# Last expert by streamed weights, two narrower expert passes, and one product of the last stage moved ahead of four transpositions

## The chip, the core and the metric

The kernel runs on one core of one Trainium2 chip, as one program that is launched once. The metric is device time in microseconds from the start of an execution to its end: 778.91 us is the median of three runs before the change (778.0 to 779.42). The engines meant below are PE (TensorE; PEld is its weight load, which overlaps its matmuls), DVE (VectorE), ACT (ScalarE), POOL (GpSimd) and SP (SyncE, which here issues most transfers). Each engine works through its own instructions in the order in which the program lists them.

## The reference

Three stages follow each other: attention, a mixture of eight experts of which each token takes one, and a dense layer with a rational function in the middle.

```python
e_idx = np.argmax(x @ w_gate, axis=1)          # x: 2304 tokens x 512, from the attention
for e in range(8):
    mask = e_idx == e
    h = np.maximum(x[mask] @ w1[e], 0.0)       # 512 -> 1024
    ye = h @ w2[e]                             # 1024 -> 512
    out[mask] = gate_w[mask, None] * eom[mask, e, None] * ye
...
h = x @ w_in                                   # 512 -> 2048
g = (a0 + a1*h + a2*h*h + a3*h**3) / (1 + |b0|*|h| + |b1|*h*h + 1e-6)
return g @ w_out                               # 2048 -> 512
```

How many tokens an expert gets follows from the inputs. With the reference's own inputs (seed 0) the eight counts are 422, 331, 253, 249, 220, 149, 434 and 118.

## The kernel before

**Precision.** Every float32 operand of a product is split in two parts, `hi` (a cast) and `lo` (the rest), and a product is made of three matmuls, hi·hi, hi·lo and lo·hi. So weights and tokens both pass an ACT cast and a subtraction on DVE or POOL before PE reads them.

**An expert pass, `wide(e, n, x, bg)`.** The tokens of expert e lie transposed in `x` (512 features by n tokens). The weights are the stationary operand, 128 columns at a time, and the n tokens are the moving one: 8 groups of 12 matmuls into `ph` (first layer) and 8 groups of 12 into four accumulators `acc` (second layer), 192 pairs of a weight load and a matmul in all, whatever n is. ACT makes the rectified `hT` of each `ph`, DVE its lo part. The width n is `WIDE.get(e, BASE)`: 296, 332, 256, 256, 256, 256, 308, 256 for the experts 0 to 7. Tokens beyond n are handled by `beyond(e)`, which stands behind a branch on the count; for the experts 0 and 6, whose tokens beyond the width are prepared in advance, it runs `single`.

**`single(e, to, x, at)`** does 128 tokens the other way round: the tokens are stationary and the weights stream past as the moving operand, 512 columns at a time (or 2 x 256 in its second half with `parts=2`): 24 matmuls for the first layer, 24 (or 48) for the second, three sets of four transpositions, and ACT and DVE work between them. Nothing is woven into it.

**What is woven into a pass.** While pass e runs, `todo` issues step by step (the table `PLANW`, 32 steps): the split of the next expert's 16 weight pieces (`s`; one ACT cast and one subtraction on DVE or POOL, alternating), the gather, scaling and transposition of the next tokens (`g`, `x`, `p`), and `c`, the conversion of 18 pieces of the last stage's weights (three DVE operations and two or three transfers each; `NCONV = 9` operations, three pieces, in each of the passes 1 to 6). Raw weights arrive in a ring of four buffers, `raw`; a buffer's next load is issued by SP once both halves in it are split.

**The last pass.** Pass 7 splits the 16 pieces of `w_in` into slot 0. `first_steps` is woven in too: it splits the first 512 tokens of the last stage (`x2_prep`, four of them, on ACT and DVE), makes the products 0 and 1 of the last stage (24 matmuls, 512 wide, into two `pt` banks) and their rational function (`first_elem`: five ACT, one POOL and five DVE operations each, then a cast and a subtraction). After the pass come `first_product(0)` (the last stage's product 2), the split of the first two pieces of `w_out` (`first_w`), a branch, and `first_product(1)`.

**The last stage** (`moe2`) has 80 steps s. PE alternates between `gemm1(s+2)`, 12 matmuls into one of two `ph` banks in the first 16 steps, and `gemm2`, which needs the finished function values. `elem(s)` is the chain on ACT, POOL and DVE between the two. A `ph` bank is free for the next product when DVE has done its second operation on it.

The functions that the change touches, as profiled:

Of the kernel before, what the change touches and what calls it, by code (L numbers as in the profile page):

```python
# [42 lines left out]
READY, WIDE = (6,), {0: 296, 1: 332, 6: 308}  # L43
# [13 lines left out]
NPRE, NCONV = 2, 9  # L57
# [3 lines left out]
PLANW = plan(32, s=range(0, 31, 2), c=(2, 3, 4, 12, 13, 14, 22, 23, 24), g=(1, 3, 18, 24), x=(1, 2, 14, 16), p=(5, 8, 19, 22))  # L61
PLANW7 = plan(30, s=(0, 5, 6, 8, 9, 11, 12, 14, 15, 17, 18, 20, 21, 23, 24, 25))
# [38 lines left out]
MODE7 = ("act",) + ("act_pool",) * 15  # L101


class Build:
# [731 lines left out]
    def experts(self, st, first, gate):  # L836
# [38 lines left out]
        def single(e, to, x, at=0, put=None, parts=2):  # L875
# [86 lines left out]
        def todo(e, plan, half=None, blocks=(), gathers=(), mode=SPLIT_MODE):  # L962
# [3 lines left out]
            k = NCONV * (e - 1)  # L966
# [26 lines left out]
        blocks = lambda e, bs=range(4): [(e, b, b) for b in bs if e < E]  # L993

# [29 lines left out]
        def expert(e, early=lambda: ()):  # L1024

            plan = PLANW if e < E - 1 else PLANW7
            more_ = blocks(e + 1, (2, 3)) if e + 1 in READY else [None] * 2
            wide(e, wd(e), X(e), weave(todo(e, plan, None, blocks(e + 1, (0, 1)) + more_, more_ + blocks(e + 2, (0, 1))),
# [65 lines left out]
        def first_steps(at=None):  # L1094

            def tick(n):
                while at and at[0] < n:
                    at[0] += 1
                    yield
            for n in range(CH[0]):  # L1100
                yield from tick(1 + n)
                self.x2_prep(n, self.x2c, n)
            h = [ps_t().tile([128, 4, 128], F32, tag="pt", name="pt").rearrange("p c t -> p (c t)") for _ in range(2)]
            gens = [self.first_elem(k, h[k], hr[k]) for k in range(2)]
            order = [("m", 0), ("m", 0), ("e", 0), ("m", 1), ("m", 1), ("e", 0), ("e", 1), ("e", 0), ("e", 1), ("e", 1)]
            parts = [self.product_parts(h[k], self.x2c, k, 512) for k in range(2)]
            for i, (c, k) in enumerate(order):
                yield from tick(8 + i + i // 2)
                next(parts[k] if c == "m" else gens[k], None)
            for k, t in enumerate(GT + (30, 30)):  # L1110
                yield from tick(t)
                next(gens[k % 2], None)
# [357 lines left out]
```

## Time and profile before

| what | value |
|---|---|
| median of the runs shown | 778.91 us |
| the profiled execution, its own time | 779.69 us |
| its span, first to last instruction | 778.0 us |
| PE busy in the span | 757.1 us (97%) |
| granted TensorE clock, mean of the span | 0.993 |
| passes 4 and 5 (experts 4 and 5), from PE's first matmul to the next pass's | 23.70 and 25.10 us |
| from pass 7's first matmul, with the block of expert 6 in it, to the last stage's first `gemm2` | 49.72 us |

The span is what the trace shows. The execution's own time is 1.7 us longer, and the median of the runs lies 0.8 us below that, so a change of the span is carried over to the median as a difference. Idle time of an engine counts only where another one waits for it; PE is the one that is nearly always busy, but what holds it back differs from stage to stage.

### The profile page before, as it was taken

The numbers are of one execution on the slowest core, as the hardware profiler recorded it, in microseconds if no ns is written. First come the engines' busy times: TensorE is split into PE (matmuls) and PEld (weight loads), VectorE is DVE, ScalarE is ACT, GpSimd is POOL, SyncE is SP. The second block draws the span as 40 slices with busy tenths as digits, with TensorE's granted clock in tenths as the row PEclk, the third lists the DMA queues.
The fourth block names the chain that finished last, engine by engine and source line by source line (L and its number), as shares of the span: only waits on it lengthen the run. The fifth ranks groups of instructions, "written<-read, shape, count | busy, mean of one in ns | idle before, by whom it ended". The sixth has DMA issues, their size and how long they took to land. (4 is left out here: it accounts for less than half of the span.)

```text
span 778.0 us, 16683 instructions
## 1 busy us (share of the span) xinstructions
PE 757.1 (97%) x5976; PEld 652.5 (84%) x5976; DVE 584.4 (75%) x1419; ACT 527.3 (68%) x1181; POOL 352.7 (45%) x439
## 2 busy tenths in 40 slices
PE   8998999899999999999999999999999999999996
PEld 5776776698999999998978888898888898989984
DVE  5777788683568877772389998888888768997983
ACT  4666775555455656643778887778777767887872
POOL 4445664523255556541756866532342214322422
PEclk9999999999999999999999999999999999999998
DMA  8998885555588999893463340110010000000101
GB/s 290 323 312 273 291 269 144 144 168 184 191 279 285 316 304 334 287 306 114 127 195 109 109 108 1 51 45 14 1 54 14 1 1 27 28 1 1 40 1 40
DMA packets 51978, 112.55 MB, mean 145 GB/s; under 512 B 10194, under 2 KB 24274, under 8 KB 49832
## 3 DMA queue, kind: packets, MB, share of 16 engines
q1 hardware_dynamic: 42232, 96.39, 39.1%
q0 software_dynamic: 3168, 9.27, 3.4%
q10 hardware_dynamic: 6480, 5.65, 2.3%
q8 instruction: 52, 0.85, 0.5%
q14 instruction: 46, 0.38, 0.2%
HBM read 93.58 MB, written 18.77 MB: 144 GB/s over the span
## 5 line engine op out<-in xcount | busy, mean ns | idle before, releaser
L1256 POOL TENSOR_TENSOR q<-q,ab 128x384 f32<-128x384 f32 (+1 forms) x78 | 93.9, 1204 | 212.1 <-ACT q L1255 205.1
L1295 PE MATMUL acc<-slot,gh 128*128 128x512 f32 x528 | 165.7, 394 | 0.0
L699 POOL TENSOR_TENSOR slot<-raw,slot 128x512 fp32r<-128x512 f32 x66 | 90.3, 1377 | 89.0 <-ACT slot L695 86.9
L1150 PE MATMUL ph<-x2c,slot 128*128 128x512 f32 (+1 forms) x552 | 125.1, 374 | 0.9 <-DVEq L1126 0.6
L1150 PEld LDWEIGHTS ph<-x2c,slot 128*128 128x128 f32 x552 | 101.1, 187 | 19.6 <-DVEq L1126 0.9
L1295 PEld LDWEIGHTS acc<-slot,gh 128*128 128x128 f32 x528 | 98.3, 187 | 20.1 <-ACT gh L1267 0.2
L944 PE MATMUL acc<-hT,slot 128*128 128x256 f32 (+3 forms) x768 | 109.2, 292 | 0.0
L1295 PE MATMUL acc<-slot,gl 128*128 128x512 f32 x264 | 104.4, 395 | 0.0
L944 PEld LDWEIGHTS acc<-hT,slot 128*128 128x128 f32 x768 | 101.9, 189 | 0.2
L695 ACT CAST slot<-raw 128x512 fp32r<-128x512 f32 x128 | 75.0, 618 | 7.6 <-DVE yt L950 4.0
L316 POOL TENSOR_SCALAR pr<-ex,r 128x128 f32<-128x128 f32 x128 | 47.0, 379 | 60.8 <-PE sc L263 21.0
L1150 PE MATMUL ph<-xa,slot 128*128 128x384 f32 x384 | 71.8, 336 | 0.0
L1150 PEld LDWEIGHTS ph<-xa,slot 128*128 128x128 f32 x384 | 67.9, 188 | 2.7
L1267 ACT CAST gh<-u 128x384 fp32r<-128x384 f32 (+1 forms) x78 | 43.3, 555 | 39.0 <-PE acc L1295 20.8
L699 DVE TENSOR_TENSOR slot<-raw,slot 128x512 fp32r<-128x512 f32 x62 | 55.0, 890 | 14.9 <-ACT slot L695 14.4
L1270 ACT ACTIVATE r<-q,cab 128x384 f32<-128x384 f32 (+1 forms) x78 | 51.3, 657 | 19.3 <-POOL q L1256 18.7
L937 ACT ACTIVATE hT<-ph 128x256 fp32r<-128x256 f32 (+3 forms) x64 | 25.7, 401 | 50.8 <-PE ph L932 40.1
L1295 PEld LDWEIGHTS acc<-slot,gl 128*128 128x128 f32 x264 | 49.4, 187 | 12.3 <-DVE gl L1268 0.3
L298 ACT ACTIVATE ex<-sm,mx 128x128 f32<-128x128 f32 x128 | 50.3, 395 | 13.9 <-POOL pr L316 7.0
L1255 ACT ACTIVATE q<-ab,cab 128x384 f32<-128x384 f32 (+1 forms) x78 | 58.3, 747 | 0.9
L1255 ACT ACTIVATE u<-ph,cab 128x384 f32<-128x384 f32 (+1 forms) x78 | 55.0, 705 | 4.0 <-POOL gl L1268 2.8
L932 PE MATMUL ph<-xa,slot 128*128 128x256 f32 (+1 forms) x384 | 54.6, 292 | 1.2 <-PEq L1040 0.4
(235 smaller groups left out, 1471.0 us busy)
## 6 DMA issues: line engine op xcount, KB each, us to landing
raw<-in_w_dram SPq DMA_DIRECT2D x78, 512.0 KB
vw<-in_vw_dram SPq DMA_DIRECT2D x16, 1024.0 KB
r<-in_w_dram SPq DMA_DIRECT2D x18, 512.0 KB
kw<-in_kw_dram SPq DMA_DIRECT2D x16, 384.0 KB
raw<-wf SPq DMA_DIRECT2D x9, 512.0 KB
qt<-in_qT_dram SPq DMA_DIRECT2D x32, 128.0 KB
xbuf<-xrow SPq DMA_DIRECT2D x8, 512.0 KB
xg<-ybuf SPq DMA_DIRECT2D x13, 256.0 KB
```

What stands on the lines that cost most here:

```text
L298: nc.scalar.activation(ex[:, h], src[:, h], AF.Exp, bias=mx[:, h:h + 1], scale=-1.0, accum_out=ssum[:, h:h + 1])
L316: nc.gpsimd.tensor_scalar(out=pr[:, h], in0=ex[:, h], scalar1=r[:, h:h + 1], scalar2=1.0, op0=ALU.mult, op1=ALU.mult)
L695: nc.scalar.copy(hi, r)
L699: eng.tensor_tensor(out=lo[:, c], in0=r[:, c], in1=hi[:, c].bitcast(F32), op=ALU.subtract)
L932: nc.tensor.matmul(ph, lhsT=W[:, b, 2 * k + s // 4, c:c + 128], rhs=x[:, a, k, :n], start=(i == 0), stop=(i == 11))
L944: nc.tensor.matmul(acc[m][:, :n], lhsT=W[:, b, 8 + f, 128 * m:128 * m + 128], rhs=hT(f % nh, n)[:, a], start=(f == 0 and i == 0), stop=(f ...
L1150: self.nc.tensor.matmul(ph[:, :w], lhsT=l[a], rhs=r[b], start=(k == 0 and i == 0), stop=(k == 3 and i == 2))
L1255: nc.scalar.activation(o_, x_, AF.Identity, scale=k1, bias=k0)
L1256: nc.gpsimd.tensor_tensor(out=q, in0=q, in1=ab, op=ALU.mult)
L1267: nc.scalar.copy(g[0], up)
L1270: nc.scalar.activation(r0, q, AF.Ln, bias=eps1)
L1295: nc.tensor.matmul(accs[i], lhsT=l[a], rhs=Wo[:, b, f, :], start=(f == 0 and j == 0), stop=(f == 15 and j == 2))
```

## The change

1. **Widths.** The passes 4 and 5 become 224 and 160 wide instead of 256. Expert 7 is prepared for 128 tokens: `pair(7)` names one block instead of two, so one gather, one scaling and one set of four transpositions with its split go from the passes 5 and 6.
2. **Conversions.** The 18 pieces are spread 4, 3, 3, 2, 2, 4 over the passes 1 to 6 instead of 3 each.
3. **Expert 7.** Its wide pass goes. After pass 6, `beyond(6)` runs at once (before, it ran after the first 12 matmuls of pass 7), and then `single(7)` with `parts=1`, into which `todo` and `first_steps` are woven by a new argument `bg`. The products 0 and 1 go into `acc3` and `acc1`, and `first_elem` keeps |h| in `yt`.
4. **Product 2** (`first_product(0)`) is issued in `single(7)` by `between`, after the second layer and ahead of the last four transpositions.
5. **Split of `w_in`**: `MODE7` gives 6 of the 16 subtractions to DVE and 10 to POOL (before: 1 and 15).

```diff
-READY, WIDE = (6,), {0: 296, 1: 332, 6: 308}
+READY, WIDE = (6,), {0: 296, 1: 332, 4: 224, 5: 160, 6: 308, 7: 128}
...
-NPRE, NCONV = 2, 9
+NPRE = 2
+PIECES = 0, 4, 3, 3, 2, 2, 4, 0
...
-PLANW7 = plan(30, s=(0, 5, 6, 8, 9, 11, 12, 14, 15, 17, 18, 20, 21, 23, 24, 25))
+PLANW7 = plan(20, s=(0, 0, 3, 3, 4, 5, 8, 9, 14, 15, 16, 16, 17, 17, 18, 18))
+ORDER1 = ((4, "m", 0), (5, "m", 0), (7, "e", 0), (8, "m", 1), (10, "e", 0), (11, "m", 1), (11, "e", 0), (12, "e", 1),
+          (13, "e", 0), (14, "e", 0), (14, "e", 1), (15, "e", 1))
...
-        def single(e, to, x, at=0, put=None, parts=2):
+        def single(e, to, x, at=0, put=None, parts=2, bg=iter(()), between=lambda: None):
...
                     if i % 3 == 2:
                         hook(n, i // 3)
+                        if i < 11:
+                            next(bg, None)
                 nc.scalar.activation(hr[n], ph, AF.Relu)
+                next(bg, None)
...
                 for k in ks:
                     hook(2, k)
+                    next(bg, None)
...
             nc.vector.tensor_copy(y[:, 256:], py[-1][:, w - 256:w])
+            between()
             pt = ps_t().tile([128, 4, 128], F32, tag="pt", name="pt")
...
+        def product_0():
+            self.bank = [ps_h.tile([128, 512], F32, tag="ph", name="ph") for _ in range(PRE)]
+            self.first_product(0)
...
         expert(E - 2, early)
-        expert(E - 1, lambda: first_steps([0]))
+        beyond(E - 2)
+        side = weave(todo(E - 1, PLANW7), first_steps([0]))
+        single(E - 1, 0, X(E - 1), parts=1, bg=side, put=put_last, between=product_0)
+        for _ in side:
+            pass
         beyond(E - 1)
-        self.bank = [ps_h.tile([128, 512], F32, tag="ph", name="ph") for _ in range(PRE)]
         first_w()
-        self.first_product(0)
```

PE, in the middle of pass 7 before: the rows L932 and L944 are the pass's own first and second layer, 256 wide, and L1150 is half of product 0 or 1.

```order
L932 MATMUL ph<-xa,slot_3377 128x256 x12
L944 MATMUL acc_6760<-hT_3406,slot_3377 128x256 x3
L944 MATMUL acc_6761<-hT_3406,slot_3377 128x256 x3
L1150 MATMUL pt<-x2c,slot_81 128x512 x6
L944 MATMUL acc_6762<-hT_3406,slot_3377 128x256 x3
L944 MATMUL acc_6763<-hT_3406,slot_3377 128x256 x3
L1150 MATMUL pt<-x2c,slot_81 128x512 x6
```

PE after the change, from behind the block of expert 6 to the end of `single(7)`: L901 is the first layer, L914 the second, L889 and L925 transpositions, L1182 the products 0 (acc_7024), 1 (acc_7071) and 2 (`ph`).

```order
L901 MATMUL acc_6986<-slot_3377,xa 128x512 x12
L901 MATMUL acc_7018<-slot_3377,xa 128x512 x3
L1182 MATMUL acc_7024<-x2c,slot_81 128x512 x6
L901 MATMUL acc_7018<-slot_3377,xa 128x512 x3
L889 MATMUL pt<-ident,hr_3407 128x128 x4
L1182 MATMUL acc_7024<-x2c,slot_81 128x512 x6
...
L1182 MATMUL acc_7071<-x2c,slot_81 128x512 x6
L914 MATMUL acc_7065<-slot_3377,hT_3406 128x512 x12
L1182 MATMUL ph<-x2c,slot_81 128x512 x12
L925 MATMUL pt<-ident,hr_3407 128x128 x4
```

The 192 matmuls of pass 7 are replaced by 48 wider ones, and the first half of product 0 now stands behind 15 matmuls instead of some 90.

ACT after the change, the first rows at the same place: L701 casts pieces of `w_in`, L1221 casts of the last stage's tokens, L906 the rectified first layer, L815 the casts of its transposed form, L1198 the first operation of product 0's function.

```order
L701 CAST slot_81<-raw_74 128x512 x2
L1221 CAST x2c<-xg_90 128x4x128
L1221 CAST x2c<-xg_91 128x4x128
L1221 CAST x2c<-xg_3385 128x4x128
L906 ACTIVATE hr_3407<-acc_6986 128x512
L701 CAST slot_81<-raw_75 128x512 x2
L1221 CAST x2c<-xg_3386 128x4x128
L701 CAST slot_81<-raw_76 128x512
L815 CAST hT_3406<-pt 128x256 x2
L701 CAST slot_81<-raw_76 128x512
L906 ACTIVATE hr_3408<-acc_7018 128x512
L1198 ACTIVATE yt<-acc_7024 128x512
```

Six pieces, four casts of tokens and four operations of expert 7 itself stand ahead of the first operation of product 0's function, and each of expert 7's waits for PE.

ACT before the change, its last rows before the last stage: L695 casts pieces of `w_in`, L1182 casts the two functions, L950 copies the pass's result, L952 and L869 are its transfers, L1117 splits `w_out`.

```order
L695 CAST slot_81<-raw_77 128x512 x2
L1182 CAST xa<-xg_91 128x2x256
L1182 CAST xa<-xg_3386 128x2x256
L950 COPY yt<-acc_6760 128x256
L950 COPY yt<-acc_6762 128x256
...
L952 DMA toks<-idxT 9x128
...
L869 DMA ybuf<-yt 128x4x256
...
L1117 CAST slot_3377<-raw_74 128x512 x2
```

The same place after the change: L920 and L926 copy the expert's result, L1146 and L875 are its transfers, L1214 is the cast of product 1's function, L1137 the split of `w_out`, L1285 the first operation of `elem(2)`.

```order
L920 COPY hr_3407<-acc_7065 128x256
L926 COPY hr_3408<-pt 128x512
...
L1146 DMA toks<-idxT 9x128
...
L875 DMA ybuf<-hr_3408 128x4x128
L701 CAST slot_81<-raw_75 128x512 x2
L1214 CAST xa<-xg_3386 128x2x256
L701 CAST slot_81<-raw_76 128x512 x2
L701 CAST slot_81<-raw_77 128x512 x2
...
L1137 CAST slot_3377<-raw_74 128x512 x2
...
L1285 ACTIVATE ab_7431<-ph 128x512
```

Six of the sixteen pieces, one cast and the split of `w_out` now stand on ACT behind the copy of the transposed result; before, the last pieces were interleaved with the pass and its result was copied last.

## Rows read from the trace of the kernel before

**Rows 1.** The page: busy time of each engine over the span.

```profile
PE 757.1 (97%) x5976; PEld 652.5 (84%) x5976; DVE 584.4 (75%) x1419; ACT 527.3 (68%) x1181; POOL 352.7 (45%) x439
```

**Rows 2.** Windows: busy us and counts, PE to POOL, then clock, DMA share, GB/s.

```profile
298.42:323.52 25.10, 24.95 (x210) 24.78 (x209) 20.30 (x31) 16.63 (x35) 16.78 (x12) 1.00 0.96 330
367.24:401.70 34.46, 33.57 (x229) 30.62 (x229) 19.07 (x31) 24.54 (x48) 23.72 (x19) 1.00 0.50 157
```

**Rows 3.** Timeline of PE in the passes 4 and 5: start us, length us, what.

```profile
289.93 1.54 PE L932 MATMUL ph<-x2c,slot 128*128 128x256 f32 x12
291.31 1.59 PE L944 MATMUL acc<-hT,slot 128*128 128x256 f32 x12
292.74 1.54 PE L932 MATMUL ph<-x2c,slot 128*128 128x256 f32 x12
...
309.72 1.60 PE L944 MATMUL acc<-hT,slot 128*128 128x256 f32 x12
311.16 1.60 PE L932 MATMUL ph<-xa,slot 128*128 128x256 f32 x12
...
315.46 0.60 PE L829 MATMUL pt<-ident,xg 128*128 128x128 f32 x4
315.82 1.68 PE L944 MATMUL acc<-hT,slot 128*128 128x256 f32 x12
```

**Rows 4.** Timeline of PE from pass 7 to the last stage.

```profile
351.98 1.60 PE L932 MATMUL ph<-xa,slot 128*128 128x256 f32 x12
353.42 4.25 PE L895 MATMUL acc<-slot,x2c 128*128 128x512 f32 x18
...
404.44 2.96 PE L1150 MATMUL ph<-x2c,slot 128*128 128x512 f32 x12
407.24 2.90 PE L1295 MATMUL acc<-slot,xa 128*128 128x512 f32 x12
...
415.57 2.96 PE L1150 MATMUL ph<-x2c,slot 128*128 128x512 f32 x12
```

**Rows 5.** Timeline of weight loads in two narrow windows, behind four transpositions.

```profile
304.87 0.19 PEld L932 LDWEIGHTS ph<-xa,slot 128*128 128x128 f32 x1
...
304.87 0.30 PEld L932 LDWEIGHTS ph<-xa,slot 128*128 128x128 f32 x2
```

**Rows 6.** Waits of SP's queue, 220 to 400 us: total, times, longest.

```profile
SPq L685 <- DVE slot L699: 90.9, 39, 13.8
```

**Rows 7.** Timeline of ACT, 359 to 398 us.

```profile
359.01 0.37 ACT L809 CAST hT<-pt 128x256 fp32r<-128x256 f32 x1 [0.49 <-DVE hT L810]
...
367.82 0.62 ACT L695 CAST slot<-raw 128x512 fp32r<-128x512 f32 x1 [0.34 <-ACTq L1040]
...
371.26 1.14 ACT L695 CAST slot<-raw 128x512 fp32r<-128x512 f32 x2
...
377.58 0.60 ACT L1166 ACTIVATE hr<-pt 128x512 f32<-128x512 f32 x1 [2.30 <-issue]
...
379.44 0.38 ACT L937 ACTIVATE hT<-ph 128x256 fp32r<-128x256 f32 x1
...
388.79 0.73 ACT L1173 ACTIVATE hr<-xg,cab 128x512 f32<-128x512 f32 x1
...
390.09 1.12 ACT L695 CAST slot<-raw 128x512 fp32r<-128x512 f32 x2
...
396.27 1.14 ACT L1117 CAST slot<-raw 128x512 fp32r<-128x512 f32 x2 [1.58 <-ACTq L1037]
398.07 0.60 ACT L1253 ACTIVATE ab<-ph 128x512 f32<-128x512 f32 x1 [0.65 <-PEq L1126]
```

**Rows 8.** Timeline of DVE: the second operation of `elem(4)` on its bank.

```profile
412.97 0.75 DVE L1260 SCALAR_TENSOR_TENSOR u<-u,cab,ph 128x512 f32<-128x512 f32 x1
```

**Rows 9.** Timeline of PE: the end of an idle stretch in the attention.

```profile
70.41 0.31 PE L368 MATMUL xv<-vw,ptg 32*32 32x64 f32 x8 [1.87 <-issue]
```

**Rows 10.** Window behind it (columns as in Rows 2).

```profile
72.00:74.00 2.00, 2.00 (x27) 1.46 (x23) 0.80 (x5) 0.52 (x2) 1.06 (x3) 0.50 0.58 58
```

More of the change, by code (lines that the diff above doesn't have):

```diff
@@ L54, in plan @@
     return o
-NPRE, NCONV = 2, 9
+NPRE = 2
+PIECES = 0, 4, 3, 3, 2, 2, 4, 0
 LOADS = [(f, f + 1) for f in range(0, NPRE, 2)] + [(f,) for f in range(NPRE, 16)]
 WLO = lambda nc, f: nc.vector if f < 3 else nc.gpsimd
-PLANW = plan(32, s=range(0, 31, 2), c=(2, 3, 4, 12, 13, 14, 22, 23, 24), g=(1, 3, 18, 24), x=(1, 2, 14, 16), p=(5, 8, 19, 22))
-PLANW7 = plan(30, s=(0, 5, 6, 8, 9, 11, 12, 14, 15, 17, 18, 20, 21, 23, 24, 25))
+EACH = {4: (2, 8, 14, 20), 3: (2, 12, 22), 2: (3, 10), 0: ()}
+PLANW = lambda e: plan(32, s=range(0, 31, 2), c=[k + n for k in EACH[PIECES[e]] for n in range(3)], g=(1, 3, 18, 24), x=(1, 2, 14, 16), p=(5, 8, 19, 22))
+PLANW7 = plan(20, s=(0, 0, 3, 3, 4, 5, 8, 9, 14, 15, 16, 16, 17, 17, 18, 18))
+ORDER1 = ((4, "m", 0), (5, "m", 0), (7, "e", 0), (8, "m", 1), (10, "e", 0), (11, "m", 1), (11, "e", 0), (12, "e", 1),
+          (13, "e", 0), (14, "e", 0), (14, "e", 1), (15, "e", 1))
+GT1 = 16, 16
+ORDER0 = tuple((0, c, int(k)) for c, k in ("m0", "m0", "e0", "m1", "m1", "e0", "e1", "e0", "e1", "e1"))
 EY = 11, 1, 11, 1
@@ L993, in experts @@
         blocks = lambda e, bs=range(4): [(e, b, b) for b in bs if e < E]
+        pair = lambda e: blocks(e, range(min(2, -(-wd(e) // 128)))) + [None] * (wd(e) <= 128)
         def fetch(e, i):
@@ L1024, in expert @@
         def expert(e, early=lambda: ()):
-            plan = PLANW if e < E - 1 else PLANW7
+            plan = PLANW(e) if e < E - 1 else PLANW7
             more_ = blocks(e + 1, (2, 3)) if e + 1 in READY else [None] * 2
-            wide(e, wd(e), X(e), weave(todo(e, plan, None, blocks(e + 1, (0, 1)) + more_, more_ + blocks(e + 2, (0, 1))),
+            wide(e, wd(e), X(e), weave(todo(e, plan, None, pair(e + 1) + more_, more_ + pair(e + 2)),
                                          iter(early())), before=(lambda: beyond(e - 1)) if e > 1 else second)
@@ L1094, in first_steps @@
         def first_steps(at=None):
+            order, late = (ORDER1, GT1) if at else (ORDER0, (0, 0))
             def tick(n):
@@ L1100, in first_steps @@
             for n in range(CH[0]):
-                yield from tick(1 + n)
+                yield from tick(n)
                 self.x2_prep(n, self.x2c, n)
[L1103 to L1110, printed above, removed]
+            h, parts, gens = {}, {}, {}
+            for t, c, k in order:
+                yield from tick(t)
+                if c == "m":
+                    if k not in h:
+                        acc = f"acc{3 - 2 * k}"
+                        h[k] = ps_a.tile([128, 512], F32, tag=acc, name=acc)
+                        parts[k] = self.product_parts(h[k], self.x2c, k, 512)
+                        gens[k] = self.first_elem(k, h[k], yt.rearrange("p m t -> p (m t)")[:, 512 * k:512 * k + 512])
+                    next(parts[k], None)
+                else:
+                    next(gens[k], None)
+            for k, t in enumerate(late + late):
                 yield from tick(t)
@@ L1118, in first_w, with put_last @@
                 nc.vector.tensor_tensor(out=lo, in0=w, in1=hi.bitcast(F32), op=ALU.subtract)
-        expert(E - 2, early)
-        expert(E - 1, lambda: first_steps([0]))
+        def product_0():
+            self.bank = [ps_h.tile([128, 512], F32, tag="ph", name="ph") for _ in range(PRE)]
+            self.first_product(0)
+        def put_last(y):
+            k = 128 - NBLK * (E - 1)
+            YQ(nc).dma_start(out=self.toks[bass.ds(off[E - 1], 128 * k), :].rearrange("(j p) o -> j (p o)", p=128),
+                             in_=self.idxT[NBLK * (E - 1):])
+            store(E - 1, 0, 128, y, YQ(nc))
+        expert(E - 2, early)
+        beyond(E - 2)
[3 more added lines that the diff above has]
+            pass
         beyond(E - 1)
-        self.bank = [ps_h.tile([128, 512], F32, tag="ph", name="ph") for _ in range(PRE)]
         first_w()
-        self.first_product(0)
         with tc.If(rare[0] > 0):
```

4 lines of the change are left out of this document (2 added, 2 removed).

## The prediction

> **What bounds the kernel now.** I read the page first: PE is busy 97% of the span [rows 1], so time can only come from less work on PE or from its few waits. Then windows by pass: in pass 5 PE is busy 24.95 of 25.10 us at full clock [rows 2], with ACT at 16.63, POOL at 16.78 and the transfers at a share of 0.96. So the passes 4 and 5 last as long as PE's 192 pairs. From pass 7's resumption to the first `gemm2` (34.46 us) PE is also nearly always busy, but ACT has 24.54 us of work there: far more than in a pass, and it does not shrink with PE's. That decides how I cost the last expert.
>
> **Narrower passes.** A group of 12 pairs at width 256 starts every 1.38 us (first layer) and 1.43 us (second) in pass 4, which is 115 and 119 ns a pair, and every 1.44 us, 120 ns, in pass 5 [rows 3]. At 512 columns a group takes 2.80 us, 233 ns a pair or 0.455 ns a column [rows 4]. If columns alone counted, 224 would take 102 ns and 160 73 ns. But each pair also loads 128 columns of weights. The trace has two loads close together only behind transpositions: one lasts 0.19 us, two span 0.30 us, so the second starts 0.11 us after the first [rows 5]. Nothing here shows narrower pairs of this kind; the bounds are 73 ns from below (no limit by loads) and today's 115 to 120 ns from above (loads already the limit). I take 110 ns for both widths, because both would be under it by their columns and a load every 110 ns is the only row that shows loads against each other. Pass 4: 117 - 110 = 7 ns x 192 = 1.3 us. Pass 5: 120 - 110 = 10 ns x 192 = 1.9 us. Pass 6 loses one set of four transpositions, 0.36 us [rows 3]. Sum 3.6 us.
>
> The shorter passes hold the same 16 splits: at 21 to 23 us they leave ACT's 16.63 and POOL's 16.78 us room [rows 2]. The transfers at 0.96 shrink too (two conversions instead of three, three gathers for four). SP's longest queue waits are for DVE to free a buffer, 90.9 us in total [rows 6]: loads wait for buffers, not the splits for loads, so I cost the transfers at nothing; if a load came late, it would delay the next pass by that much. The third and fourth conversions moved into pass 1 and pass 6 add three DVE operations to each, which I cost at nothing beside PE's work there.
>
> The Trainium skill, in "TensorE: Matmul & The Clock Gate" (section Back-to-back issue gap), gives about 81 ns a pair for 128 columns in a sustained stream; if 160 columns took that, pass 5 would gain 7.5 us by my estimate. No row here shows so short a pair, and the 110 ns between loads speak against it.
>
> **Expert 7 by streamed weights.** PE's work falls: 180 pairs of 120 ns go (the first 12 ran before the block of expert 6, so that block also starts 353.42 - 351.98 = 1.44 us earlier [rows 4]), 48 of 233 ns and twelve transpositions come, some 9 us less. But the engines behind it decide, in program order. I set T = 0 at PE's start of `single(7)`, which is 367.24 - 1.44 = 365.80 on the clock of before [rows 2, 4]; ACT starts 0.58 later [rows 7].
>
> ACT's work up to `elem(2)`: 22 casts of pieces, tokens and `w_out`, one every 0.52 us, 11.4; two functions of 1.86 + 1.30 us, 6.3; two casts of their results 1.0; four casts of `hT` of 0.37, 1.5; two rectified rows of 0.6, 1.2; the result's copies 1.0; its stores and the branch 1.6; the second branch 0.65 [rows 7]. Sum 24.7 us.
>
> ACT's waits, by walking the new order with these durations:
> - The first half of product 0 needs the fourth cast of tokens, now ninth on ACT (T = 5.3), and its lo part (T = 6.1). PE has issued 15 matmuls by T = 3.5 and idles about 2 us. Its transpositions come at T = 8.0, and ACT, done with its tenth job at 5.8, waits 2.8 us for them.
> - Twice 0.5 us for DVE between two `hT` casts [rows 7], 1.0 for the second rectified row (PE is 12 matmuls further on), 0.6 for the second transpositions, 0.5 for DVE's result of the first function.
> - 2.4 us near the end: the last transpositions need DVE's half of the result's copy, which stands in DVE's queue behind both functions (T = 25.2). Behind the copy, ACT still has the stores, six pieces, a cast and `w_out`.
> Together 8.3 us. So `elem(2)` starts at T = 0.6 + 24.7 + 8.3 = 33.6, or 399.4 on the old clock; before it started at 398.07 [rows 7]. It is 1.3 us **later**, although PE has 9 us less to do.
>
> PE itself reaches `gemm2(0)` when `w_out` is split, about T = 33, 398.8; before 401.70 [rows 2]. It cannot keep those 2.9 us. In the first 16 steps a product needs a bank that `elem` has freed, and the chain of `elem` paces itself. Its tightest place before is step 4: DVE frees the bank at 412.97 + 0.75 = 413.72 [rows 8] and PE takes it at 415.57 [rows 4], a slack of 1.85 us. With `elem` 1.3 us later PE can gain 1.85 - 1.3 = **0.55 us**. Its bounds: 8.3 us more, if none of the waits were there, and a loss without limit as the waits grow.
>
> Product 2 ahead of the transpositions fills 2.8 us of PE in which it would wait for the result's copy; since ACT sets the end, I cost the move at nothing, and without it `first_product(0)` would run in PE's idle time before `w_out` is ready. The new split between DVE and POOL only has to keep the pieces ahead of PE: DVE gets five more subtractions, before the result's copy only two of them.
>
> **Sum.** 1.3 + 1.9 + 0.36 + 0.55 = 4.1 us off a span of 778.0 us, 773.9. The profiled execution took 779.69 and the median of the runs is 778.91; I subtract from the median: **774.8 us**.
>
> **The rivals.**
> 1. *Columns decide in the narrow passes* (chance 0.05). Pass 4 gains (117 - 102) x 192 = 2.9 us, pass 5 (120 - 73) x 192 = 9.0 us; in all 12.8 us off, 766.1. For it: 233 ns at 512 and 115 at 256 are nearly in proportion. Against it: the 110 ns between loads. The Trainium skill's page named above would have pass 5 nearly so.
> 2. *Loads already decide at 256* (0.12). The passes give nothing, 0.9 us is left, 778.0. For it: 120 ns in pass 5 where columns alone ask for 116.5. Against it: 115 ns in the first layer of pass 4.
> 3. *ACT waits half as much* (0.13). Four us more, 770.7. For it: my walk takes every wait in full.
> 4. *The clock falls in PE's idle 2 us* (0.12). In the attention PE idled 1.87 us [rows 9], and soon after the granted clock was 0.50, the lower of its two levels (1.2 of 2.4 GHz), for a whole window of 2 us [rows 10]. Matmuls at half speed while ACT waits for them would shift `elem(2)` by up to 1.7 us: 776.5. The later idle stretches, some 2.6 and 3.6 us, stand before `elem(2)` and cost PE alone, which has 2.3 us to spare.
> 5. *Slower* (0.10). The last expert is now a serial chain through PE, ACT, DVE and POOL where before it was a pass beside which ACT worked freely. If each of its handovers takes as long again as I count, 8.3 us more, the time is 783.1. It is slower than before from 4.1 us of extra wait on.
> If the tokens did not fit the new widths, an extra block of about 13.8 us (from 353.42 to 367.24 [rows 2, 4]) would run for that expert. The counts 220, 149 and 118 fit 224, 160 and 128, and the profile of before shows such a block for the experts 0 and 6 alone, as these counts ask for; I give it no chance of its own.
>
> **How the numbers follow.** The likeliest case, 4.1 us off give or take 2, has 0.48 and lies at 773 to 777. The difference that this kernel's runs can tell from none is 0.2%, 1.56 us. Faster by more than that: the likeliest case, rivals 1 and 3 and most of 4 and a third of 2, together 0.79. Within 0.2%: the rest of 2 and a part of 4, 0.11. Slower: rival 5, 0.10. The range leaves out rival 1, rival 5 and the far half of 3: 769.5 to 778.3.
>
> **What would show it.** In the profile after: pairs of the passes 4 and 5 start every 110 ns, and both passes last about the same but for transpositions, 21.5 to 23 us. At 75 ns in pass 5 rival 1 holds, at 118 rival 2. In the last expert PE idles about 2 us before the first half of product 0, and again before the last transpositions and before `gemm2(0)`. `elem(2)` starts 33 to 34 us after `single(7)` does. The prediction is wrong if PE keeps its 9 us, which would need ACT to be done by T = 25, or if PE waits in the first 16 steps beyond the first three.

## The result, and the profile after

The changed kernel is slower by 1.4%: 790.02 us, median of six runs (786.88 to 808.78), against 778.45 for the kernel before (776.36 to 779.88). The ratio is 1.0144, with a 95% interval of 1.0116 to 1.0173. Some executions, here the one of 808.78 us, run 13 to 25 us longer at a lower clock; they are in the medians and left out of each ratio.

The page and the windows by stage show where the time went (columns as in [rows 1, 2]). PE has less work, 750.2 us for 757.1, and the span is still 11.6 us longer.

```profile
PE 750.2 (95%) x5840; PEld 640.2 (81%) x5840; DVE 589.6 (75%) x1418; ACT 523.2 (66%) x1177; POOL 342.8 (43%) x433
```

The windows of the changed kernel are, in order, the passes 2, 3, 4 and 5, then `single(7)` up to the first `gemm2`, then the rest of the last stage:

```profile
225.89:250.50 24.61, 23.86 (x202) 23.49 (x201) 18.07 (x27) 14.32 (x31) 12.70 (x10) 1.00 0.87 291
250.50:281.98 31.48, 25.80 (x202) 25.02 (x201) 20.41 (x32) 14.64 (x31) 13.34 (x10) 0.97 0.77 251
281.98:305.29 23.31, 23.16 (x202) 23.01 (x201) 17.46 (x26) 13.01 (x27) 12.22 (x9) 0.97 0.88 281
305.29:329.59 24.30, 23.71 (x211) 23.28 (x209) 18.91 (x28) 16.77 (x37) 14.83 (x12) 1.00 0.92 307
371.85:413.30 41.45, 29.00 (x109) 21.92 (x110) 23.86 (x34) 25.90 (x47) 18.31 (x14) 0.79 0.42 135
413.30:789.60 376.30, 369.40 (x1729) 315.91 (x1727) 310.72 (x512) 285.34 (x500) 151.51 (x141) 0.99 0.11 35
```

The kernel before had, for the passes 2 and 3 and for the last stage (its pass 5 and last expert are [rows 2]; pass 4 took 23.70 us):

```profile
226.72:250.47 23.75, 23.60 (x202) 23.43 (x201) 19.39 (x29) 14.42 (x31) 12.57 (x11) 1.00 0.88 293
250.47:274.72 24.25, 24.10 (x202) 23.93 (x201) 19.04 (x29) 14.28 (x31) 13.90 (x11) 1.00 0.92 312
401.70:778.00 376.30, 369.38 (x1729) 315.92 (x1727) 309.90 (x513) 288.34 (x502) 151.72 (x141) 0.99 0.12 36
```

So 0.86 + 7.23 us were lost in the passes 2 and 3, which the prediction had left out, and 41.45 - 34.46 = 6.99 in the last expert. The passes 4 and 5 gave back 0.39 and 0.80, pass 6 some 0.4, the block of expert 6 with the 12 pairs ahead of it 1.0; what comes ahead of pass 2 took 0.8 us less. The last stage takes the same 376.30 us. These add up to the 11.6.

**Pass 3.** The rows of the timeline that belong together, by their start (DVE, ACT's and SP's queues, PE; L737 is the first operation of a conversion, L875 the transfer of the pass's result, L761 the transfer of a converted piece, L949 DVE's lo part of `hT`):

```profile
252.26 0.39 ACTq L875 DMA_DIRECT2D ybuf<-yt  x1
261.71 0.43 DVE L737 TENSOR_SCALAR yt<-r 128x512 int32<-128x512 int32 x1 [5.18 <-DMA ybuf<-yt]
262.79 0.42 DVE L949 SCALAR_TENSOR_TENSOR hT<-ph,hT 128x256 fp32r<-128x256 f32 x1
263.26 1.69 PE L943 MATMUL ph<-xa,slot 128*128 128x256 f32 x12 [1.94 <-DVE hT L949]
271.03 0.33 SPq L761 DMA_DIRECT2D wf<-f  x1
276.66 1.97 DVE L737 TENSOR_SCALAR f<-r 128x512 int32<-128x512 int32 x1 [2.87 <-DMA wf<-f]
279.74 2.44 PE L955 MATMUL acc<-hT,slot 128*128 128x256 f32 x10 [3.06 <-DVE hT L949]
```

A conversion writes one of two buffers: `f`, or a part of `yt`, in which the pass before it left its result. Which one is settled by the piece's number (`self.f32[q % 3 % 2]`, a line that the diff does not touch): with three pieces in each pass the order is f, yt, f, and the `yt` piece stands in the middle of the pass. With four pieces in pass 1 the numbers shift by one: the passes 2, 3 and 4 begin with `yt`, and in the passes 2 and 3 then come two `f` in a row. The result's transfer, issued at 252.26, frees `yt` at 261.71 only, 9.4 us later; a piece's transfer, issued at 271.03, frees `f` at 276.66. (In pass 4 the first `yt` piece, at 289.25, waited only 1.77 us, and for its raw data; the stall does not come each time that it could.) DVE works in order, so the lo part of `hT` waits behind the conversion, and PE behind DVE.

**The last expert.** The rows of the timeline of PE, then ACT, DVE and POOL:

```profile
377.17 0.51 PE L1182 MATMUL acc<-x2c,slot 128*128 128x512 f32 x1 [1.60 <-ACT x2c L1221]
378.04 1.85 PE L1182 MATMUL acc<-x2c,slot 128*128 128x512 f32 x5 [0.36 <-DVE x2c L1222]
398.86 0.44 PE L925 MATMUL pt<-ident,hr 128*128 128x128 f32 x2 [1.40 <-DVE hr L921]
405.86 0.79 PE L1182 MATMUL ph<-x2c,slot 128*128 128x512 f32 x1 [6.57 <-ACTq L1158]
408.73 4.73 PE L1182 MATMUL ph<-x2c,slot 128*128 128x512 f32 x11 [2.07 <-DVEq L1158]
413.30 2.92 PE L1327 MATMUL acc<-slot,xa 128*128 128x512 f32 x12
...
404.63 1.14 ACT L1137 CAST slot<-raw 128x512 fp32r<-128x512 f32 x2 [0.17 <-ACTq L1050]
407.52 0.60 ACT L1285 ACTIVATE ab<-ph 128x512 f32<-128x512 f32 x1 [1.75 <-DMA xg<-xbuf,idx]
...
401.37 0.69 DVE L705 TENSOR_TENSOR slot<-raw,slot 128x512 fp32r<-128x512 f32 x1 [2.57 <-ACT slot L701]
403.68 3.43 DVE L705 TENSOR_TENSOR slot<-raw,slot 128x512 fp32r<-128x512 f32 x2
407.32 1.29 DVE L1138 TENSOR_TENSOR slot<-raw,slot 128x512 fp32r<-128x512 f32 x2 [0.21 <-DVEq L1050]
...
403.50 3.06 POOL L705 TENSOR_TENSOR slot<-raw,slot 128x512 fp32r<-128x512 f32 x2 [0.29 <-ACT slot L701]
```

From the last transpositions (398.86) to 405.86 PE has nothing to do. Product 3 (`first_product(1)`) stands behind the branch L1158, whose body would write its operands again; so its first matmul waits for ACT to reach the branch, behind the cast of `w_out` (404.63 + 1.14), and its second for DVE, behind the subtraction of `w_out` (407.32 + 1.29). And the matmuls that do come are slow: 11 in 4.73 us. The granted clock (third column from the right) in two stretches, each of which begins just after PE has idled:

```profile
378.90:382.20 3.30, 3.30 (x11) 2.66 (x10) 0.00 (x0) 0.14 (x1) 1.45 (x2) 0.50 0.43 134
399.40:412.90 13.50, 4.96 (x11) 3.59 (x12) 9.28 (x10) 8.68 (x15) 5.62 (x4) 0.50 0.70 234
```

It was 0.50, the lower level of 1.2 GHz, in both. The first stretch begins in the first half of product 0, the second holds product 3.

In the kernel before, the same wait at the same branch is there as well, and short. Product 2 stood between pass 7 and the branch there, and no piece of `w_in` was left to split; the experiment on product 2 shows which of the two counted:

```profile
399.03 2.83 PE L1150 MATMUL ph<-x2c,slot 128*128 128x512 f32 x11 [0.59 <-DVEq L1126]
```

### The profile page after: what moved, and what is told of

It reads as the page before. It is cut to its first block, busy times and chain, and to the rows that moved or that the text cites. A ratio compares the mean times of both kernels' runs of the same rounds, so it can differ in the third digit from the quotient of the medians.

```text
span 789.6 us, 16393 instructions
## 1 busy us (share of the span) xinstructions
PE 750.2 (95%) x5840; PEld 640.2 (81%) x5840; DVE 589.6 (75%) x1418; ACT 523.2 (66%) x1177; POOL 342.8 (43%) x433
## 5 line engine op out<-in xcount | busy, mean ns | idle before, releaser
L1182 PE MATMUL ph<-x2c,slot 128*128 128x512 f32 (+1 forms) x552 | 127.2, 379 | 8.6 <-ACTq L1158 6.6
L705 POOL TENSOR_TENSOR slot<-raw,slot 128x512 fp32r<-128x512 f32 x61 | 82.7, 1360 | 108.3 <-ACT slot L701 108.0
L1182 PEld LDWEIGHTS ph<-x2c,slot 128*128 128x128 f32 x552 | 102.8, 190 | 27.7 <-ACTq L1158 6.8
L955 PE MATMUL acc<-hT,slot 128*128 128x256 f32 (+5 forms) x672 | 96.0, 293 | 3.7 <-DVE hT L949 3.7
L955 PEld LDWEIGHTS acc<-hT,slot 128*128 128x128 f32 x672 | 89.5, 191 | 4.1 <-DVE hT L949 4.1
L701 ACT CAST slot<-raw 128x512 fp32r<-128x512 f32 x128 | 75.1, 617 | 15.2 <-DVE yt L961 5.3
L705 DVE TENSOR_TENSOR slot<-raw,slot 128x512 fp32r<-128x512 f32 x67 | 61.4, 921 | 17.8 <-ACT slot L701 17.3
L1182 PE MATMUL ph<-xa,slot 128*128 128x384 f32 x384 | 71.8, 336 | 0.0
L1182 PEld LDWEIGHTS ph<-xa,slot 128*128 128x128 f32 x384 | 67.9, 188 | 2.7
L948 ACT ACTIVATE hT<-ph 128x256 fp32r<-128x256 f32 (+5 forms) x56 | 21.7, 387 | 51.4 <-PE ph L943 39.4
L1292 DVE SCALAR_TENSOR_TENSOR u<-u,cab,ph 128x384 f32<-128x384 f32 (+1 forms) x78 | 51.9, 666 | 2.8
```

Source lines behind the costliest of these rows:

```text
L701: nc.scalar.copy(hi, r)
L705: eng.tensor_tensor(out=lo[:, c], in0=r[:, c], in1=hi[:, c].bitcast(F32), op=ALU.subtract)
L955: nc.tensor.matmul(acc[m][:, :n], lhsT=W[:, b, 8 + f, 128 * m:128 * m + 128], rhs=hT(f % nh, n)[:, a], start=(f == 0 and i == 0), stop=(f ...
L1182: self.nc.tensor.matmul(ph[:, :w], lhsT=l[a], rhs=r[b], start=(k == 0 and i == 0), stop=(k == 3 and i == 2))
L1292: nc.vector.scalar_tensor_tensor(out=u, in0=u, scalar=a1, in1=h, op0=ALU.add, op1=ALU.mult)
```

## The experiments

The theory: two causes, independent of each other. The table of pieces shifts the buffers (some 8 us, theory of the shared buffer), and product 3 behind the branch with late splits ahead of it leaves PE idle at the end (some 7 us, theory of the branch). Rivals: the widths or the mere number of conversions cause the stall in pass 3; the chain of ACT alone sets the end; the lower clock is the cost.

Three kernels make one part of the change alone, the fourth repairs one place.

**The pieces alone**, in the kernel before:

```diff
-c=(2, 3, 4, 12, 13, 14, 22, 23, 24)
+c=[k + n for k in EACH[PIECES[e]] for n in range(3)]     # PIECES = 0, 4, 3, 3, 2, 2, 4, 0
...
```

> The kernel before, with the conversions spread 4, 3, 3, 2, 2, 4 over the passes 1 to 6 as its only change. The theory of the shared buffer: the conversion cycles through two buffers, and with four pieces in pass 1 the first piece of the passes 2 and 3 meets the one that still holds the result of the pass before, so DVE stands behind that result's transfer and PE behind DVE. Then pass 2 is 0.9 us and pass 3 some 5 to 7 us longer than before, 784 to 787 us against 778.5. The rival, that those waits came from something else in the changed kernel: no difference, 778 to 779.

787.76 us, ratio 1.0127 (1.0095 to 1.0159). Its windows of the passes 2 and 3, and the two waits of DVE for a transfer there (us in total, times, longest), neither of which the kernel before has:

```profile
225.48:252.20 26.72, 23.95 (x203) 23.58 (x201) 19.95 (x29) 14.31 (x31) 12.63 (x10) 1.00 0.81 274
252.20:282.75 30.55, 25.48 (x203) 24.90 (x201) 19.99 (x30) 14.65 (x31) 13.34 (x10) 0.97 0.77 253
...
DVE yt L733 <- DMA ybuf<-yt: 6.1, 2, 4.6
DVE f L733 <- DMA wf<-f: 5.4, 2, 2.8
```

The table of pieces costs 2.97 + 6.30 us in these two passes, some four fifths of the whole loss. DVE's wait for the result's transfer makes one half of it, its wait at the second `f` in a row the other. The time is 0.8 us above the range expected.

**The widths alone**, in the kernel before:

```diff
-{0: 296, 1: 332, 6: 308}
+{0: 296, 1: 332, 4: 224, 5: 160, 6: 308}
```

> The kernel before, with the passes 4 and 5 at 224 and 160 as its only change. If a pair at either width takes the 112 ns that the changed kernel shows, pass 4 loses some 1 us and pass 5 some 1.5 us: 775.5 to 776.5 against 778.5. If shorter passes bring DVE or the transfers late, part of it is lost: 777 to 779. If the widths caused the stall in pass 3, slower than before.

778.11 us, ratio 0.9984 (0.9963 to 1.0006): between a gain of 2.9 us and a loss of 0.5. In the profile, pass 4 takes 22.68 us and pass 5 23.79, 1.02 and 1.31 less than before, and pass 3 stays at 24.25. So the widths do not cause the stall; the gain in the passes is near what was expected, but the median is above its range, and the runs can't tell it from nothing.

**The last expert alone** (the changed kernel with `PIECES = 0, 3, 3, 3, 3, 3, 3, 0` and the widths of the passes 4 and 5 back at 256):

> The changed kernel with three conversions in each pass and the passes 4 and 5 back at 256: expert 7 by streamed weights and product 2 ahead of the transpositions stay. The theory that the new last stretch is by itself 7 us longer: its stretch from the start of the last expert to the first product of the last stage's second layer stays at 41 us, the block of expert 6 starts 1 us earlier, and the time is 783 to 785 us, 5 to 6 us over before. The rival, that the stretch was long only because what came ahead of it was late: 776 to 779.

783.41 us, ratio 1.0068 (1.0051 to 1.0084), as expected. The stretch takes 39.79 us. It is long by itself, whatever comes ahead of it. Ahead of product 0 PE idles the same 1.60 and 0.36 us as in the changed kernel, but this time the clock stayed at 1.00 there; at the end it fell again, to 0.50:

```profile
371.00:378.20 7.20, 6.83 (x32) 5.42 (x32) 1.39 (x3) 2.63 (x7) 4.22 (x3) 1.00 0.27 87
391.60:404.90 13.30, 5.30 (x12) 3.84 (x13) 9.61 (x11) 8.45 (x15) 5.62 (x4) 0.50 0.73 223
...
371.59 1.43 PE L1182 MATMUL acc<-x2c,slot 128*128 128x512 f32 x5 [0.36 <-DVE x2c L1222]
395.35 3.42 DVE L705 TENSOR_TENSOR slot<-raw,slot 128x512 fp32r<-128x512 f32 x2
399.19 0.60 ACT L1285 ACTIVATE ab<-ph 128x512 f32<-128x512 f32 x1 [1.75 <-DMA xg<-xbuf,idx]
```

That clock is what sets the two apart: `elem(2)` starts 399.19 - 365.41 = 33.78 us after `single(7)` here and 407.52 - 371.85 = 35.67 in the changed kernel, and 1.6 us of the difference are there already when DVE copies the expert's result (at 24.9 and 26.5).

The three parts by themselves, +1.27, -0.16 and +0.68%, make 1.8% where the whole makes 1.44. The stalls vary: the passes 2 to 4, with the same code, took 79.4 us in the changed kernel's profiled execution and 78.5, 81.1 and 82.9 in three kernels below that leave them as they are.

**Product 3 ahead of the branches**, in the changed kernel:

```diff
+        self.first_product(1)
         beyond(E - 1)
         first_w()
         with tc.If(rare[0] > 0):
...
             self.first_product(0)
-        self.first_product(1)
+            self.first_product(1)
```

> The changed kernel with product 3 moved from behind the branch to just behind the last expert's last transpositions. The theory of the branch: product 3 waits until ACT and DVE have both reached the branch, so moving it fills PE's idle stretch and the last stage's first second-layer product starts 4 to 5 us sooner, 785 to 786 us against 790.0. The rival, that the chain of ACT up to the function of step 2 decides, whatever PE does: a gain of under 1 us, 789 to 790.

788.35 us, ratio 1.0113 (1.0092 to 1.0135), measured beside the three above. PE's first product of the second layer:

```profile
409.49 4.50 PE L1328 MATMUL acc<-slot,xa 128*128 128x512 f32 x12 [6.71 <-ACT u L1288]
```

The stretch falls by 4.7 us, to 36.76, as the theory of the branch wanted, but the 785 to 786 us expected were missed: the time falls by some 2 us, and its interval and that of the changed kernel overlap. PE now idles 6.7 us at once, and for ACT: moving product 3 leaves the chain of ACT as the limit. The clock falls, the first 12 matmuls of the last stage's second layer take 4.50 us and not 2.92, and the last stage takes 1.6 us longer (377.9). What comes ahead of the last expert took 0.9 us more; the passes 2 and 3 vary (27.63 and 26.68 here).

**The buffers in turn again**, in the changed kernel, first for the passes 2 and 3 (pieces 4 to 9), then also for pass 4 (pieces 10 and 11):

```diff
-        self.conv_op(self.r64[q % 2], self.f32[q % 3 % 2], n)
+        f = self.f32[(q - (4 <= q < 10)) % 3 % 2]           # second kernel: 4 <= q < 12
+        self.conv_op(self.r64[q % 2], f, n)
...
```

> The changed kernel with one edit: the six pieces of the passes 2 and 3 take the conversion's two buffers in the order f, yt, f again, as before, while the number of pieces in each pass stays 4, 3, 3, 2, 2, 4. The theory of the shared buffer: the waits of DVE for the result's transfer go, the passes 2 and 3 fall back to 23.8 and 24.3 us, and the time falls by some 8 us, 781 to 783 against 790.0. The rival, that the number of DVE operations or their transfers are the cause and not the buffer they meet: 787 to 791.

785.26 us, ratio 1.0101 (1.0055 to 1.0146). The passes 2 and 3 are back at 23.85 and 24.25 us, and the stall stands in pass 4. Its first piece met `yt` early in the changed kernel as well, where it waited little. Its window, and ACT's issue of the result with DVE's wait:

```profile
272.18:300.45 28.27, 24.41 (x202) 24.08 (x201) 16.74 (x26) 13.33 (x29) 12.59 (x10) 0.94 0.77 250
...
272.94 0.39 ACTq L876 DMA_DIRECT2D ybuf<-yt  x1
...
284.54 0.43 DVE L737 TENSOR_SCALAR yt<-r 128x512 int32<-128x512 int32 x1 [7.38 <-DMA ybuf<-yt]
```

The buffer theory is right about the mechanism; the time was missed because the same collision was overlooked one pass further on. In the last expert the clock stayed up during product 0: `elem(2)` comes at 33.76 us, the stretch takes 39.22.

> The changed kernel with the conversion's buffers taken in the order f, yt from the first piece of pass 2 to the last of pass 4, so that in none of these passes the first piece meets the buffer that holds the result; nothing else changes. With only passes 2 and 3 mended, pass 4 had taken over the wait (28.3 us). The theory of the shared buffer: pass 4 falls to 22 to 23 us as well and the time to 779.5 to 781.5, what is left over before being the last stretch. If the wait then turns up in pass 5 or 6, or the transfers are the cause: 784 or more.

781.97 us, ratio 1.0035 (1.0013 to 1.0057): by the ratio 781.1, within what was expected, by the median 0.5 above it. The execution that was profiled took 799.57 us, with nearly all of the excess in pass 5; the rows are those of the passes 2 to 4, at full clock:

```profile
224.89:248.65 23.76, 23.61 (x203) 23.44 (x202) 18.90 (x29) 14.43 (x31) 12.67 (x10) 1.00 0.89 300
248.65:272.90 24.25, 24.10 (x202) 23.93 (x201) 19.03 (x29) 14.22 (x31) 13.89 (x11) 1.00 0.93 312
272.90:296.11 23.21, 22.79 (x203) 22.45 (x201) 17.57 (x26) 12.88 (x28) 13.27 (x10) 1.00 0.87 301
```

With the number of conversions unchanged at 4, 3, 3, 2, 2, 4, the loss in these passes is gone, 1.0144 - 1.0035, some 8.5 us. The kernels below with the same turn of the buffers take 23.75, 24.26 and 22.7 to 23.1 us in them. So it was the buffer and not the number of operations or of transfers.

**The idle stretch filled** with 24 superfluous matmuls, in the changed kernel (`self.first_product(1)` twice more, ahead of `beyond(E - 1)`):

> The changed kernel with 24 superfluous matmuls of 512 columns (product 3 computed twice ahead of time, its results overwritten) behind the last expert's last transpositions, ahead of the branch: 5.6 us of work in an idle stretch of PE of 6.6 us. Product 3 itself stays behind the branch. If the lower clock after the idle stretch costs time, the clock stays at its full level there, product 3 takes 2.9 us and not 4.7, and the time falls by 1.5 to 2 us, to 788 to 788.5. If the clock costs nothing there because ACT and DVE decide: 789.5 to 790.5. If the fillers come in the way of product 3: slower than 791.

789.27 us, ratio 1.0154 (1.0109 to 1.0198): no difference from the changed kernel. The clock fell all the same, at 399.30, behind the 1.40 us ahead of the fillers, and once more at 409.54; the stretch took 40.85 us. It tells nothing about the clock's share.

**Product 2 behind the transpositions again** (`between()` two statements later):

> The changed kernel with product 2 put behind the last four transpositions, as the order was before the change. If the order of the two makes no difference, because the transpositions wait for DVE's copy and what follows waits for the branch: 789.5 to 790.5. If product 2 ahead of them costs what it makes the result's copy wait: faster by 1 to 2 us. If it shortens PE's idle stretch from behind and so keeps the clock up: faster by up to 2 us as well, with the granted clock at its full level until product 3.

792.13 us, ratio 1.0183 (1.0144 to 1.0221). It overlaps with the changed kernel's interval, and its profiled execution differs from that one mostly by the stalls in the passes 2 to 4 (82.9 us for 79.4). A difference under 2 us stays open. The stretch takes 40.15 us with product 0 at full clock, where the two kernels above that kept it so took 39.79 and 39.22: one execution each, in favour of product 2 ahead. Behind the transpositions product 2 does not cover the branch: PE still waits there, and product 3 is as slow.

```profile
408.59 0.49 PE L1182 MATMUL ph<-x2c,slot 128*128 128x512 f32 x1 [2.12 <-ACTq L1158]
411.46 4.79 PE L1182 MATMUL ph<-x2c,slot 128*128 128x512 f32 x11 [2.38 <-DVEq L1158]
```

So it is ACT and DVE that come late to it, behind the splits and the copy.

**The splits earlier**, with the passes 2 and 3 mended and product 3 ahead of both branches:

```diff
-s=(0, 0, 3, 3, 4, 5, 8, 9, 14, 15, 16, 16, 17, 17, 18, 18)
+s=(0, 0, 3, 3, 4, 4, 4, 4, 4, 4, 8, 8, 10, 12, 14, 15)
...
-MODE7 = ("act",) * 2 + ("act_pool",) * 6 + ("act", "act_pool") * 4
+MODE7 = ("act",) * 2 + ("act_pool",) * 2 + ("act_pool", "act") * 4 + ("act_pool",) * 4
```

> The changed kernel with three repairs: the buffers of the passes 2 and 3 as before, product 3 ahead of the branch, and the splits of the pieces 4 to 15 issued earlier, into ACT's idle 4.4 us ahead of the first transpositions and among the functions, so that none stands behind the result's copy. If the late splits, by ACT and by DVE beside POOL, are what holds the function of step 2 and the first product of the second layer, this stretch falls from 41 us to 33 and the time to 773 to 776, 3 to 5 us under the kernel before. If the chain of the expert and the two functions decides whatever stands behind it: the stretch stays at 36 to 37 us and the time is 777 to 780.

780.24 us, ratio 1.0016 (0.9988 to 1.0043): neither of the two. The stretch takes 35.09 us, but pass 4 still stalls (28.06), and a new wait stands at the end: ACT's split of `w_out` overwrites weights that the body of the branch on expert 7's tokens would read, so it waits until PE has passed that branch, and PE came late to it because of product 3.

```profile
400.18 1.14 ACT L1138 CAST slot<-raw 128x512 fp32r<-128x512 f32 x2 [3.48 <-PEq L1051]
```

**Product 3 between the branches**, the buffers of pass 4 mended and its second piece two steps later, the splits as in the kernel above:

> The kernel with earlier splits, with the buffers of pass 4 mended too, its second piece one step pair later, and product 3 between the two branches and not ahead of both. In the run before this, ACT's split of w_out waited 3.5 us for PE to reach the first branch, behind product 3. If that wait goes, the first product of the second layer comes 32 to 33 us after the last expert's start, not 35, and with pass 4 at 23 us the time is 772 to 774. If ACT then waits as long for something else: 775 to 777.

774.45 us, ratio 0.9958 (0.9939 to 0.9978): 0.4% faster than before. The wait at the first branch is gone, but ACT now waits 2.62 us for PE at the second, behind product 3, as the second case of the expectation had it. The stretch takes 34.80 us: the clock fell during product 0 again, and product 3 ran for 5.37 us at the lower clock behind 1.44 and 1.75 us of idle PE.

```profile
395.48 0.60 ACT L1287 ACTIVATE ab<-ph 128x512 f32<-128x512 f32 x1 [2.62 <-PEq L1160]
404.90 3.06 PE L1184 MATMUL ph<-x2c,slot 128*128 128x512 f32 x12 [0.74 <-DVE u L1294]
```

The second row is new: PE now waits for a bank that `elem` has to free.

**The copy of the result ahead of product 1's function** (its last two steps moved from 14 and 15 to 16), with three splits moved too:

> The kernel of the run just above, with the last steps of product 1's function put behind the copies of the last expert's result, and the splits of three pieces moved behind the first transpositions, where DVE's split of the transposed result had waited for DVE's other splits. If the result's copy in DVE's queue and the idle stretches that it makes on PE are what is left of the loss, the first product of the second layer comes 27 to 30 us after the last expert's start and the time is 768 to 772, about 1% under the kernel before. If the function of product 1, now later, holds the second step of the last stage: 772 to 775.

776.00 us, ratio 0.997 (0.9949 to 0.9991). The stretch falls to 33.30 us, but PE then idles 4.72 us in one piece, and the first second-layer product takes 5.46 us. Nothing was gained over the kernel above, and the expectation was missed.

**Product 3 straight behind product 2, without and with a filler.** The filler is a product into an unused bank between the branches.

```diff
             self.first_product(0)
+            self.first_product(1)
...
```

Buffers and splits are those of the kernel with product 3 between the branches.

> The kernel with product 3 behind the first branch, but product 3 now straight behind product 2, ahead of the last four transpositions, so that PE works while DVE's copy of the result is late. The clock theory: PE no longer idles 1.4 and 1.75 us there, product 3 takes 2.9 us and not 5.4, and the first product of the second layer comes 32.5 to 33.5 us after the last expert's start, not 34.8; the time is 772 to 774. PE's idle stretch behind the transpositions is then 3 to 4 us long, and a lower clock may follow it and cost up to 1.7 us in the last stage. If ACT and DVE decide alone: 34.5 us or more and 774 to 775.

773.67 us, ratio 0.9954 (0.9934 to 0.9974), the lowest median of all, though its interval hardly differs from that of the kernel with product 3 between the branches. The stretch takes 31.64 us; some 1.6 of the 3.2 less were gained ahead of product 2, where the clock stayed up during product 0 this time. PE's rows:

```profile
381.54 5.76 PE L1184 MATMUL ph<-x2c,slot 128*128 128x512 f32 x24
...
393.02 4.63 PE L1329 MATMUL acc<-slot,xa 128*128 128x512 f32 x12 [4.20 <-DVEq L1160]
...
400.29 2.90 PE L1329 MATMUL acc<-slot,xa 128*128 128x512 f32 x12
```

Both products run at full clock, and the clock falls in the 4.20 us of idle PE; the 12 matmuls after it cost 4.63 - 2.90 = 1.73 us more than the next 12 of the same kind.

> The kernel of the run just above with 12 superfluous matmuls of 512 columns into an unused bank between the two branches (their result is read by nobody), 2.8 us of work in PE's idle stretch of 3 to 4 us. The clock theory: the granted clock stays at its full level from there on, and the time is 1 to 1.7 us lower than in the run just above. If the clock falls all the same or costs nothing: no difference; if the fillers hold back the first product of the second layer: up to 1 us slower.

776.84 us, ratio 0.9976 (0.9952 to 0.9999). The intervals overlap; by the medians it is slower than without the filler. The filler itself waited 1.86 us at the first branch, ran at the lower clock and held ACT up at the second (3.58 us), and the second layer came at 35.52 us; 1.6 of the 3.9 more lie ahead of the filler, where the clock fell during product 0. So the fillers do not show what the clock costs at the end. The rows show that it depends on who is last: the 1.73 us above cost nothing, since `elem` paces PE there (the table below), while in the kernel with the copy first the end comes 379.9 us after `elem(2)` and not 378.1, for which the slow product of 5.46 us, 2.5 longer than at full clock, can account.

## Why the prediction was wrong

**The step that failed first** is the sentence "The third and fourth conversions moved into pass 1 and pass 6 add three DVE operations to each, which I cost at nothing beside PE's work there." The operations do cost nothing: with the buffers in turn, the same spread runs without a stall. But the table also renumbers every later piece, and the number chooses the buffer. This line is outside the diff, and I asked of the moved instructions only how long they take, not which memory they touch and who else is using it. It cost about 8 us, in passes that the prediction did not look at.

**The second failed step** is "PE itself reaches `gemm2(0)` when `w_out` is split, about T = 33". It counted the work ahead of `gemm2(0)` and forgot product 3, which can't start until ACT and DVE are at the branch: `gemm2(0)` began at T = 41.45. ACT and DVE come there late, behind the splits that now follow the result's copy. Part of that is DVE beside POOL: the rule that a split "only has to keep the pieces ahead of PE" took no account of it. DVE's last two subtractions lasted 3.43 us together while POOL did two of its own (403.50, 3.06 us), where the one at 401.37, begun with POOL idle, lasted 0.69; some 2 us, by this estimate, of what product 3 waited for DVE. The Trainium skill, in "SBUF — State Buffer" (section Who interferes with whom), says that a DVE instruction with two SBUF inputs contends with a GpSimd instruction that reads SBUF; the trace agrees.

**The third** is the clock, rival 4, in both its halves. "Matmuls at half speed while ACT waits for them would shift `elem(2)` by up to 1.7 us" had a chance of 0.12, and happened: `elem(2)` came at 35.67, 2.1 later than forecast, and 1.6 of that are the clock during product 0, since with the clock up there it came at 33.78 and 33.76, though DVE's two subtractions beside POOL took as long there (3.42 and 3.43 us). Of eleven profiled executions with the new last expert (the one of 799.57 us aside), the clock fell there in five and stayed up in six, behind the same idle time of PE. The other half is wrong: the later idle stretches "cost PE alone, which has 2.3 us to spare". The clock stayed at 0.50 for 13.5 us behind them, and product 3, which `gemm2(0)` waits for, ran in it: 4.73 us for 11 matmuls that took 2.83 before.

Where PE or `elem` sets the end is seen by counting from `elem(2)`, all in us (T = 0 is the start of `single(7)`):

| kernel | `elem(2)` at T | `gemm2(0)` at T | from `elem(2)` to the end |
|---|---|---|---|
| forecast | 33.6 | 33 | 379.9 - 1.85 = 378.1 |
| before | 32.3 | 35.9 | 379.9 |
| changed | 35.7 | 41.5 | 382.1 |
| last expert alone | 33.8 | 39.8 | 382.3 |
| product 3 between the branches | 34.7 | 34.8 | 378.1 |
| copy first | 32.5 | 33.3 | 379.9 |
| product 3 straight behind product 2 | 32.3 | 31.6 | 378.2 |
| the same with a filler | 35.4 | 35.5 | 378.1 |

In the changed kernel PE is 4.0 us behind what `elem` would allow. The forecast's last column is right, once product 3 is out of the way: PE can use the slack of 1.85 us at the bank and no more.

**What held.** The pairs: a group of 12 starts every 1.34 us in both widths, 112 ns a pair, for the 110 that was taken from the gap between two loads; neither rival 1 nor rival 2. From PE's timeline of pass 4 and pass 5:

```profile
293.21 1.50 PE L955 MATMUL acc<-hT,slot 128*128 128x224 f32 x12
294.55 1.51 PE L943 MATMUL ph<-x2c,slot 128*128 128x224 f32 x12
...
316.46 1.50 PE L955 MATMUL acc<-hT,slot 128*128 128x160 f32 x12
317.80 1.50 PE L943 MATMUL ph<-xa,slot 128*128 128x160 f32 x12
```

By the widths alone the passes gave 1.02 and 1.31 us, for 1.3 and 1.9 forecast. The 81 ns of the Trainium skill, in "TensorE: Matmul & The Clock Gate" (section Back-to-back issue gap), were not reached at either width here. The walk through ACT's chain held: 1.60 + 0.36 us of idle PE for "about 2" and, where the clock stayed up, DVE's half of the result's copy at 24.9 for 25.2 and `elem(2)` at 33.8 for 33.6. So close a sum is luck in part: ACT stood 1.75 us ahead of `elem(2)`, where the sum has 0.65 for the second branch. That the move of product 2 alone makes no difference was neither shown nor refuted in the time.

Rival 5 had the sign, but not the places: its handovers came 2 us late, by the clock, and not 8, and of the 11.6 us most came from a buffer and a branch that no rival named. A gain of about the size forecast, 4.1 us, is there once both are mended and the splits moved: the kernel with product 3 straight behind product 2 runs at 773.67 us, 4.3 under the 777.96 of the kernel before beside it (2.0 to 5.1 by its interval). It is another kernel than the one forecast, so the agreement proves nothing of the sum.

## What to carry to other kernels

Where a table moves steps of a cycle that takes buffers by a running number, list for each step which buffer it gets and who used that buffer last, before and after: the numbers shift for all steps behind the one that was added. At a branch, look for the engine that comes to it last: a wait of 0.59 us there became 6.57 + 2.07 us when splits came to stand ahead of it on ACT and DVE, and putting the product that had stood there back left 2.12 + 2.38. When PE no longer sets the end, fill its idle time with the useful work that comes next; the fillers tried here gained nothing. Compare two variants of a stretch only where the clock did the same in both.

## What the runs showed of the hardware that was not expected

- A transfer of a result, 256 columns, from `yt` to `ybuf` held its buffer for 9.4 us (252.26 to 261.71) and in another kernel for 11.6 us (272.94 to 284.54) after its issue, with the transfers at a share of 0.77 in these passes. At the same place it was 8.0 us in the kernel with product 3 ahead of the branches (256.11 to 264.08).
- The granted clock does not follow the idle time alone: behind the same 1.60 and 0.36 us of idle PE it fell to 0.50 in the changed kernel and stayed at 1.00 in the kernel with the last expert alone. Behind the longest idle stretches (4.20 us and more, in six kernels) it was at 0.50 each time.
